# A three-layer kernel on one core: a weight block's conversion moved behind the fourth attention unit, and the second token group's sums ranked later, half of their low parts on VectorE

## The chip, the cores and the metric

The kernel runs on one core of one Trainium2 chip. The metric is the device time of one execution in microseconds (us): the median of three runs.

## What is computed

Attention with a memory term over 2 batches, 8 heads, 576 positions and 64 columns per head, then two feed-forward stages over the 1152 tokens that come out:

```python
scores = scale * np.matmul(q, k.transpose(0, 1, 3, 2))      # causal, softmax -> a
local = np.matmul(a, v)
mem_out = einsum(phi(q), M_prev) / einsum(phi(q), z_prev)
attn = g * mem_out + (1 - g) * local                        # (2, 8, 576, 64)
x = attn.transpose(0, 2, 1, 3).reshape(1152, 512)
h = x @ w_in                                                # 512 -> 2048
x = np.where(h > 0, h, np.exp(np.minimum(h, 0)) - 1) @ w_out
out = 0
for e in range(4):                                          # 512 -> 1024 -> 512 each
    out += p[:, e:e+1] * (np.maximum(x @ w1[e], 0) @ w2[e])
```

## The kernel before

Every float32 product is made of three float32r matmuls (`mm3`, lines 277 to 280): high times high, low times high, high times low. So each operand is split into a high part (a ScalarE copy) and a low part (a subtraction, mostly on GpSimd, which the profile calls POOL).

The tokens are in two groups. Group 0 (384 tokens) comes from four small attention units, `F0` to `F3`, one for each pair of heads. Group 1 (768 tokens) comes from eight larger ones, `R00` to `R13`. `Moe1` and `Moe2` are the two feed-forward stages of group 0. Their matmuls run while the `R` units are still worked out, in gaps of one another. Then `Wide1` and `Wide2` do group 1 with Winograd's scheme of seven products for eight, which needs sums of token quarters (`T1` to `T4`, each in two halves `kk`) and sums of weight quarters (`s32`).

An attention unit makes scores (`sF`, `sR`, banks `s0` and `s1` or `m`), row minima on VectorE (`lowest`, line 1311), exponentials on ScalarE, transposes (`tF`, `tR`), copies of them (`pf`, line 1364 on VectorE), products with the values (`sums`), the scaling of the result (`sum_a`, `sum_i`, `sum_f`: lines 1223, 1438, 1229), the sum with the memory term (`both`, line 1416) and a last transpose (`turn`, tile `xF` or `xR`), which is split into `xh` and `xl`.

A weight block `i` is 128 x 1024. The first sixteen come as 64-bit words, in two halves `w64_i_0` and `w64_i_1`, and are converted: ScalarE `upper` (line 225), VectorE `shift` (231) and `lower` (235), which give the block `wr`. ScalarE then makes its high part `wh` (245), and POOL its low part `wl` (249). The first three blocks are converted in place in `wr`; the others go through the PSUM banks `s0` and `s1` that the scores use too. Those later blocks wait in the plan for `GATE`, one of the scores of `F3` (`score20`). Weight blocks 0 and 1 are for the first upward products (`ua`), 2 and 3 for the first downward ones (`da`).

The order on every engine is set by a planner, `Plan.order`: it plays through the steps with guessed costs, and each time an engine is free takes the step of lowest rank whose inputs and buffers are there. Only the order goes into the program; on the chip each engine runs its queue in that order and waits where it must. Where the planner sees TensorE wait for over 0.3 us in the first 140 us of its own clock, `keep_busy` puts matmuls of zeros (`nothing`, line 304) ahead of the step, into the PSUM tile that the step will write:

```python
waits[0] = min(int(IDLE * wait / 0.22) + 1, IDLE_MAX)
```

The downward results of group 0's first stage share three PSUM banks, tag `m`: of the last part, `da0300`, `da0310` and `da0320` hold all three until VectorE has made their low parts (`yl`, line 457), and `da0330` takes the first that comes free.

Of the kernel before, what the change touches and what calls it, by code (L numbers as in the profile page):

```python
# [54 lines left out]
def f32(ap):  # L55
    return ap.bitcast(F32)
# [3 lines left out]
def tile_kernel(  # L60
# [12 lines left out]
    nc = tc.nc  # L73
# [80 lines left out]
    W_EARLY = 3  # L154
# [14 lines left out]


    FEWEST = {"F": 1, "R": 0}
    GATE = ("F3", "score20")
    UNIT1 = 5.0
    EARLY = 4.0
    START2 = 48.0
    STARTS2 = [0, 35, 70, 95, 110, 125, 140, 155]
# [11 lines left out]
    def plan_weights(plan, i, rank):  # L188

        second, k = divmod(i, NW1 + NW2)  # L190
        t = {}
        last = [None]

        def add(name, engine, cost, fn, takes=(), gives=()):
            plan.add(("w", i, name), engine, cost, rank, fn, [last[0]] if last[0] else (), takes, gives)
            last[0] = ("w", i, name)

        def block():
            t["wr"] = wp.tile([P, 1024], F32, tag="wr", name=f"wr{i}", bufs=SLOTS["wr"])

        def load():
            block()
            if k >= NW1:
                nc.sync.dma_start(out=t["wr"], in_=w32[k - NW1])
            elif second:
                nc.sync.dma_start(out=t["wr"], in_=wscr[k])

        def load64(half):
            cs = slice(512 * half, 512 * half + 512)
            raw = at["sbuf"].tile([P, 512], I64, tag=f"w64_{half}", name=f"w64_{i}_{half}", bufs=SLOTS["w64_0"])  # L210
            nc.sync.dma_start(out=raw, in_=w64[i, :, cs])
            words = raw.bitcast(I32).rearrange("p (n two) -> p n two", two=2)
            t[half] = words[:, :, 0], words[:, :, 1]

        def upper(half):
            if half == 0:
                block()
            _, high = t[half]

            if i < W_EARLY:  # L220
                t["cv", half] = t["wr"][:, 512 * half:512 * half + 512]
            else:
                t["cv", half] = abank(f"s{half}", f"cv{i}_{half}")

            nc.scalar.activation(
                out=t["cv", half], in_=high.bitcast(F32), func=AF.Prelu, scale=2.0 ** -112, alpha=2.0 ** 32
            )

        def shift(half):
            c = t["cv", half].bitcast(I32)  # L230
            nc.vector.tensor_scalar(out=c, in0=c, scalar1=3, scalar2=None, op0=ALU.logical_shift_left)

        def lower(half):
            low, wi = t[half][0], t["wr"][:, 512 * half:512 * half + 512].bitcast(I32)
            nc.vector.scalar_tensor_tensor(
                out=wi, in0=low, scalar=29, in1=t["cv", half].bitcast(I32),
                op0=ALU.logical_shift_right, op1=ALU.bitwise_or,
            )

        def keep():  # L240
            nc.sync.dma_start(out=wscr[i], in_=t["wr"])

        def part_h():
            t["wh"] = wp.tile([P, 1024], F32R, tag="wh", name=f"wh{i}")
            nc.scalar.activation(out=t["wh"], in_=t["wr"], func=AF.Copy)  # L245

        def part_l():
            wl = wp.tile([P, 1024], F32R, tag="wl", name=f"wl{i}")
            nc.gpsimd.tensor_tensor(out=wl, in0=t["wr"], in1=f32(t["wh"]), op=ALU.subtract)  # L249
            wtiles[i] = (t["wh"], wl)  # L250

        if k < NW1 and not second:
            ends = []
            for half in range(2):
                last[0] = None
                add(f"load{half}", "sync", 1.6, lambda half=half: load64(half), [f"w64_{half}"])
                bank = [] if i < W_EARLY else [f"s{half}"]
                plan.add(
                    ("w", i, f"upper{half}"), "act", act_cost(512), rank, lambda half=half: upper(half),
                    [last[0]] + [GATE] * (i >= W_EARLY) + [("w", i, "upper0")] * half, bank + ["wr"] * (half == 0),  # L260
                )
                last[0] = ("w", i, f"upper{half}")
                add(f"shift{half}", "dve", dve_cost(512), lambda half=half: shift(half))
                ends.append(("w", i, f"lower{half}"))
                plan.add(
                    ends[-1], "dve", dve_cost(512), rank, lambda half=half: lower(half), [last[0]], [],
                    [f"w64_{half}", *bank],
                )
            plan.add(("w", i, "keep"), "sync", 1.6, rank + 3.0, keep, [*ends, ("w", i, "part_l")], gives=[("wr", ("w", i, "upper0"))])
            plan.add(("w", i, "part_h"), "act", act_cost(1024), rank, part_h, ends, ["w"])  # L270
            last[0] = ("w", i, "part_h")
        else:
            add("load", "sync", 1.6, load, ["wr"])
            add("part_h", "act", act_cost(1024), part_h, ["w"])
        add("part_l", "pool", pool_cost(1024), part_l, gives=[("wr", ("w", i, "load"))] * (k >= NW1 or second))
# [391 lines left out]
    class Halves:  # L667
# [29 lines left out]
                self.sums[name] = hp[0].tile([P, 2, 384], F32, tag="t32", name=f"{self.what}{name}", bufs=SLOTS["t32"])  # L697
            fn(self.sums[name][:, kk])

        def plan_parts(self, plan, rank, name, kk, gives=()):  # L700
            def high():
                nc.scalar.activation(out=self.tile(name, "h")[:, kk], in_=self.sums[name][:, kk], func=AF.Copy)

            def low():
                nc.gpsimd.tensor_tensor(
                    out=self.tile(name, "l")[:, kk], in0=self.sums[name][:, kk],
                    in1=f32(self.tile(name, "h")[:, kk]), op=ALU.subtract,
                )

            plan.add((self.what, name + "h", kk), "act", act_cost(384), rank, high, [(self.what, name, kk)])  # L710
            plan.add((self.what, name + "l", kk), "pool", pool_cost(384), rank, low, [(self.what, name + "h", kk)], [], gives)

        def plan(self, plan, rank, ready):

            for name, x, y in (("T1", "B12", "B11"), ("T2", "B22", "T1"), ("T3", "B22", "B12"), ("T4", "B21", "T2")):
                for kk in (0, 1):
                    def subtract(out, x=x, y=y, kk=kk):
                        nc.vector.tensor_tensor(
                            out=out, in0=self.quarter(x)[:, kk], in1=self.quarter(y)[:, kk], op=ALU.subtract
                        )  # L720

                    after = [a for n in (x, y) for a in ([(self.what, n, kk)] if n[0] == "T" else ready(n, kk))]
                    plan.add(
                        (self.what, name, kk), "dve", dve_cost(384), rank,
                        lambda name=name, kk=kk, fn=subtract: self.total(name, kk, fn), after, ["t32"] * (kk == 0),
                    )
                    self.plan_parts(plan, rank, name, kk, ["t32"] * kk)

    keep = {}

# [299 lines left out]
    def dve_cost(n):  # L1030
        return 1.042e-3 * n + 0.115

    def pool_cost(n):
        return 2.1e-3 * n + 0.2
# [418 lines left out]
    x1 = Halves("x", lambda: x32)  # L1453
# [12 lines left out]
    with ExitStack() as first, tc.manual_schedule():  # L1466
        attention_pools(attention, first)
        ps_m = first.enter_context(tc.tile_pool(name="ps_m", bufs=SLOTS["m"], space=PSUM, reuse_waits="tile"))

        ps = at["t"].tile([P, 512], F32, tag="t", name="warm")  # L1470
        for i in range(WARM):
            nothing(ps)
        plan, clock = Plan(SLOTS), [START2]
        plan.awake, plan.last = IDLE_END, 0.43 * WARM - 0.5
        plan_small(plan, OFFSET["load"] + 3.0, 1.5)
        for c in range(H // 2):
            plan_unit(plan, "F", None, c, UNIT1 * c, True, {})
        for i in range(W_FIRST):
            plan_weights(plan, i, W_RANKS[i])
        wnext[0] = W_FIRST  # L1480
        units = [(b, c) for c in range(H // 2) for b in (0, 1)]
        for (b, c), start in zip(units, STARTS2):
            plan_unit(plan, "R", b, c, START2 + start, False, {"act": 0.3, "dve": 0.1, "pool": 0.3, "pe": 0.3})
        Moe1(plan, 0, 0, clock).layers()
        Moe2(plan, 0, NW1, clock).layers()
        x1.plan(plan, START2 + STARTS2[-1] + 8.0, lambda name, kk: [(f"R{b}{c}", "join_l") for b, c in units])
        free = plan.order({"pe": 0.43 * WARM - 0.5})
    ps_g = ctx.enter_context(tc.tile_pool(name="ps_g", bufs=8, space=PSUM, reuse_waits="tile"))
    with tc.manual_schedule():
        plan, clock = Plan(SLOTS | {"m": 8, "h": 4}), [free["pe"]]  # L1490
# [91 lines left out]
```

## Time and profile before

| | |
|---|---|
| median of 3 runs | 728.83 us (728.65 to 729.18) |
| the profiled execution | 729.03 us, of which 727.2 us are the span from its first to its last instruction |
| TensorE busy | 717.5 us (99%) |
| VectorE, ScalarE, POOL busy | 396.7, 354.2, 425.7 us |
| mean granted TensorE clock | 0.995 |

Times of rows are microseconds from the span's start. A row of the order of time gives start, duration and, in brackets, the idle time of the engine just before it and who ended it. PE is TensorE, DVE is VectorE, ACT is ScalarE. Tiles stand there without their numbers (`da` for `da0330`, `w` for `w64_2_0`).

### The profile page before, as it was taken

The numbers are of one execution on the slowest core, as the hardware profiler recorded it, in microseconds if no ns is written. First come the engines' busy times: TensorE is split into PE (matmuls) and PEld (weight loads), VectorE is DVE, ScalarE is ACT, GpSimd is POOL, SyncE is SP. The second block draws the span as 40 slices with busy tenths as digits, with TensorE's granted clock in tenths as the row PEclk, the third lists the DMA queues.
The fourth block names the chain that finished last, engine by engine and source line by source line (L and its number), as shares of the span: only waits on it lengthen the run. The fifth ranks groups of instructions, "written<-read, shape, count | busy, mean of one in ns | idle before, by whom it ended". The sixth has DMA issues, their size and how long they took to land.

```text
span 727.2 us, 11034 instructions
## 1 busy us (share of the span) xinstructions
PE 717.5 (99%) x4255; PEld 643.9 (89%) x4255; DVE 396.7 (55%) x846; ACT 354.2 (49%) x610; POOL 425.7 (59%) x256
## 2 busy tenths in 40 slices
PE   9989999999999999998999999999999999999997
PEld 5768998888889888897999999998998989899896
DVE  4887785434353443435537474873635546364562
ACT  7768877454444543444568373753323324243130
POOL 5468688665536442259878763597656456664210
PEclk9999999999999999999999999999999999999999
DMA  7677985434233041221423021112312203021002
GB/s 260 214 267 266 388 294 165 143 106 136 87 108 109 31 138 32 85 91 55 159 88 116 30 87 59 59 33 84 116 40 77 88 29 117 30 88 58 1 1 87
DMA packets 23541, 80.36 MB, mean 110 GB/s; under 512 B 2881, under 2 KB 2881, under 8 KB 23489
## 3 DMA queue, kind: packets, MB, share of 16 engines
q1 hardware_dynamic: 23488, 79.66, 32.6%
q8 instruction: 33, 0.54, 0.3%
q14 instruction: 20, 0.16, 0.1%
HBM read 68.90 MB, written 10.75 MB: 110 GB/s over the span
## 4 chain that ended last, share of the span: by engine, by line
PE 96%; POOL 2%; DVE 1%; issue 0%; ACT 0%
PE db L278 9%; PE db L280 9%; PE db L279 9%; PE sums L1375 5%; PE da L278 5%; PE da L279 5%; PE da L280 5%; PE ub L278 3%; PE sR L1297 3%; PE ub L280 3%; PE ub L279 3%; PE tR L1359 3%; PE sums L1384 2%; PE ua L278 2%; PE ua L280 2%; PE ua L279 2%
## 5 line engine op out<-in xcount | busy, mean ns | idle before, releaser
L249 POOL TENSOR_TENSOR wl<-wr,wh 128x1024 fp32r<-128x1024 f32 x72 | 171.9, 2391 | 178.7 <-ACT wh L245 140.0
L245 ACT ACTIVATE wh<-wr 128x1024 fp32r<-128x1024 f32 x72 | 75.7, 1056 | 96.5 <-PE db L279 55.8
L278 PE MATMUL db<-wh,hb 128*128 128x512 f32 x288 | 115.6, 401 | 0.0
L280 PE MATMUL db<-wl,hb 128*128 128x512 f32 x288 | 113.4, 394 | 2.2 <-POOL wl L249 2.2
L279 PE MATMUL db<-wh,hb 128*128 128x512 f32 x288 | 113.0, 392 | 0.0
L997 DVE SCALAR_TENSOR_TENSOR acc<-db,pr,acc 128x512 f32<-128x512 f32 x42 | 31.5, 751 | 70.0 <-PE db L280 69.2
L280 PEld LDWEIGHTS db<-wl,hb 128*128 128x128 f32 x288 | 54.4, 189 | 14.3 <-POOL wl L249 2.6
L278 PE MATMUL da<-ha,wh 128*128 128x384 f32 x192 | 65.1, 339 | 0.0
L278 PEld LDWEIGHTS db<-wh,hb 128*128 128x128 f32 x288 | 54.5, 189 | 11.9 <-issue 1.4
L280 PE MATMUL da<-ha,wh 128*128 128x384 f32 x192 | 64.2, 334 | 0.0
L279 PE MATMUL da<-ha,wl 128*128 128x384 f32 x192 | 64.2, 334 | 0.0
L279 PEld LDWEIGHTS db<-wh,hb 128*128 128x128 f32 x288 | 54.5, 189 | 10.3
L278 PE MATMUL ub<-yh,wh 128*128 128x384 f32 x128 | 46.3, 362 | 0.0
L280 PE MATMUL ub<-yl,wh 128*128 128x384 f32 x128 | 43.1, 336 | 0.0
L279 PE MATMUL ub<-yh,wl 128*128 128x384 f32 x128 | 43.0, 336 | 0.0
L1375 PE MATMUL sums<-rvR,pfR 128*128 128x65 f32 x288 | 37.4, 271 | 0.0
L278 PEld LDWEIGHTS da<-ha,wh 128*128 128x128 f32 x192 | 36.1, 188 | 0.7 <-issue 0.4
L1375 PEld LDWEIGHTS sums<-rvR,pfR 128*128 128x128 f32 x288 | 35.3, 191 | 1.0
L279 PEld LDWEIGHTS da<-ha,wl 128*128 128x128 f32 x192 | 36.1, 188 | 0.0
L280 PEld LDWEIGHTS da<-ha,wh 128*128 128x128 f32 x192 | 36.0, 188 | 0.0
L537 DVE SCALAR_TENSOR_TENSOR acc<-db,pr,acc 128x512 f32<-128x512 f32 x21 | 15.7, 749 | 36.4 <-PE db L280 36.3
L1320 ACT ACTIVATE ptR<-ptR,nmR 128x576 f32<-128x576 f32 (+2 forms) x48 | 29.9, 659 | 10.2 <-DVE nmR L1311 10.2
(860 smaller groups left out, 1838.1 us busy)
## 6 DMA issues: line engine op xcount, KB each, us to landing
wr<-in_w SPq DMA_DIRECT2D x64, 512.0 KB, 3.5
w<-in_w SPq DMA_DIRECT2D x32, 512.0 KB, 5.8
wscr<-wr SPq DMA_DIRECT2D x16, 512.0 KB, 6.9
wr<-wscr SPq DMA_DIRECT2D x16, 512.0 KB, 3.3
qkR<-in_qk_r SPq DMA_DIRECT2D x8, 480.0 KB, 5.0
rvR<-in_vm_r SPq DMA_DIRECT2D x8, 390.0 KB, 4.0
out<-acc SPq DMA_DIRECT2D x8, 256.0 KB, 2.0
qkF<-in_qk_f SPq DMA_DIRECT2D x4, 416.0 KB, 3.8
```

The source lines that it names most:

```text
L245: nc.scalar.activation(out=t["wh"], in_=t["wr"], func=AF.Copy)
L249: nc.gpsimd.tensor_tensor(out=wl, in0=t["wr"], in1=f32(t["wh"]), op=ALU.subtract)
L278: nc.tensor.matmul(out, ah, bh, start=first, stop=False)
L279: nc.tensor.matmul(out, al, bh, start=False, stop=False)
L280: nc.tensor.matmul(out, ah, bl, start=False, stop=last)
L537: nc.vector.scalar_tensor_tensor(out=acc, in0=t["ps"], scalar=p, in1=acc, op0=ALU.mult, op1=ALU.add)
L997: nc.vector.scalar_tensor_tensor(out=acc, in0=t["ps"], scalar=p, in1=acc, op0=ALU.mult, op1=ALU.add)
L1297: nc.tensor.matmul(unit["s", odd, t, n][:, :w], unit[x][rows, q], unit[y][rows, ks[odd]], start=m == 0 and r0 == 0, stop=m == 2 and final,)
L1320: nc.scalar.activation(out=blk, in_=blk, func=AF.Exp, scale=-1.0, bias=unit["nm"][odd][:, k:k + 1])
L1359: nc.tensor.transpose(pst[:, P * n:P * n + P], src, ident)
L1375: nc.tensor.matmul(unit["ov"][:, odd, t], pf[:, col:col + P], unit["rv"][:, at_], start=j == 0, stop=False)
L1384: nc.tensor.matmul(unit["ov"][r0:r0 + r, o, t], pf[rows, col + r0:col + r0 + r], unit["rv"][rows, at_], start=nb == 0, stop=True,)
```

## The change

Three edits. The third block (`i` is 2, the last that is converted in place) now waits in the plan for `sum_f` of `F3`, where it waited for nothing but its load. The token sums of group 1 get the rank of the end of group 0's layers less 15 (in the planner's clock some 20 us later than before). The low parts of `T1` and `T4` are made on VectorE, and those of `T2` and `T3` stay on POOL. The gates and ranks are only the planner's: no wait is added to the program, but the order of all engines changes from there on, in the first 175 us above all.

```diff
+    GATE_IN_PLACE = ("F3", "sum_f")
...
+                gate = [GATE] if i >= W_EARLY else [GATE_IN_PLACE] if i >= 2 else []
                 plan.add(
                     ("w", i, f"upper{half}"), "act", act_cost(512), rank, lambda half=half: upper(half),
-                    [last[0]] + [GATE] * (i >= W_EARLY) + [("w", i, "upper0")] * half, bank + ["wr"] * (half == 0),
+                    [last[0]] + gate + [("w", i, "upper0")] * half, bank + ["wr"] * (half == 0),
                 )
...
-        def plan_parts(self, plan, rank, name, kk, gives=()):
+        def plan_parts(self, plan, rank, name, kk, gives=(), on_dve=False):
...
+            eng, cost = (nc.vector, ("dve", dve_cost(384))) if on_dve else (nc.gpsimd, ("pool", pool_cost(384)))
...
-                nc.gpsimd.tensor_tensor(
+                eng.tensor_tensor(
                     out=self.tile(name, "l")[:, kk], in0=self.sums[name][:, kk],
...
-                    self.plan_parts(plan, rank, name, kk, ["t32"] * kk)
+                    self.plan_parts(plan, rank, name, kk, ["t32"] * kk, name in ("T1", "T4"))
...
-        x1.plan(plan, START2 + STARTS2[-1] + 8.0, lambda name, kk: [(f"R{b}{c}", "join_l") for b, c in units])
+        x1.plan(plan, clock[0] - 15.0, lambda name, kk: [(f"R{b}{c}", "join_l") for b, c in units])
```

In the listings of the order below, numbers behind the last underscore are the program's buffers, and line numbers after the edit are 1 to 4 higher.

**First place: VectorE at the end of the attention unit `F3`.** Before, a shift of block 2 stands between the scaling of `F3`'s memory term (`nm_F3`) and the copy `pfF31` of its last transposes:

```order
L1229 TENSOR_TENSOR sums_120<-sums_120,nm_F3_633 128x2x3x64
L231 TENSOR_SCALAR wr2_550<-wr2_550 128x512
L1364 COPY pfF31_654<-tF31_644 128x384
L1430 TENSOR_TENSOR xl0_101<-xF2_639,xh0_100 128x384
L235 SCALAR_TENSOR_TENSOR wr2_550<-w64_2_0_371,wr2_550 128x512
L231 TENSOR_SCALAR wr2_550<-wr2_550 128x512
L1223 SCALAR_TENSOR_TENSOR nv_F3_673<-sums_120,wloc_96 128x6
```

After the change:

```order
L1233 TENSOR_TENSOR sums_120<-sums_120,nm_F3_630 128x2x3x64
L1368 COPY pfF31_650<-tF31_640 128x384
L1434 TENSOR_TENSOR xl0_101<-xF2_636,xh0_100 128x384
L1227 SCALAR_TENSOR_TENSOR nv_F3_662<-sums_120,wloc_96 128x6
L1442 RECIPROCAL nv_F3_662<-nv_F3_662 128x6
L1233 TENSOR_TENSOR tvF3_665<-sums_120,nv_F3_662 128x2x3x64
L1420 TENSOR_TENSOR tvF3_665<-tvF3_665,sums_120 128x384
L232 TENSOR_SCALAR wr2_669<-wr2_669 128x512
L236 SCALAR_TENSOR_TENSOR wr2_669<-w64_2_0_371,wr2_669 128x512
```

The copy now follows the scaling at once, and all four instructions of block 2 stand behind `F3`'s `both`.

**Second place: TensorE at the end of group 0's first stage.** Before, `da0330` follows `da0320`, whose last quarter has the inputs `ha033`:

```order
L278 MATMUL da0320_1784<-ha033_1655,wh15_1543 128x384
L279 MATMUL da0320_1784<-ha033_1655,wl15_1547 128x384
L280 MATMUL da0320_1784<-ha033_1655,wh15_1543 128x384
L278 MATMUL da0330_1811<-ha030_1437,wh15_1543 128x384
```

After the change (the pair of zeros is there five times):

```order
L282 MATMUL da0320_1811<-ha033_1719,wh15_1562 128x384
L1301 MATMUL sR01001_1834<-qhR01_1585 128x288
L1301 MATMUL sR01101_1835<-qhR01_1585 128x288
L1301 MATMUL sR01001_1834<-qlR01_1601,qhR01_1585 128x288
L1301 MATMUL sR01101_1835<-qlR01_1601,qhR01_1585 128x288
L1301 MATMUL sR01001_1834<-qhR01_1585,qlR01_1601 128x288
L1301 MATMUL sR01101_1835<-qhR01_1585,qlR01_1601 128x288
L306 LDWEIGHTS zeros_93
L306 MATMUL da0330_1854<-zeros_93 128x384
```

On VectorE the low part of `da0300`, which frees a bank for `da0330`, now stands behind the row minima of those scores:

```order
L448 TENSOR_TENSOR da0300_1777<-da0300_1777,xr0_852 128x384
L448 TENSOR_TENSOR da0310_1798<-da0310_1798,xr0_852 128x384
L448 TENSOR_TENSOR da0320_1811<-da0320_1811,xr0_852 128x384
L1315 ISA ptR01_1745,nmR010_1746<-sR01001_1834,mask_71,nmR010_1746 128x288
L1315 ISA nmR010_1746 128x1
L459 TENSOR_TENSOR yl0_1844<-da0300_1777,yh0_1843 128x384
```

Part of `R01`'s scores moved ahead of `da0330`, and five matmuls of zeros were put there. In all the program has 18 matmuls of zeros behind the first upward product `ua0000` where it had 6: 5 before the scores `sR00001`, 3 before `da0000`, 2 before the scores `sR10000`, 3 before `da0200` and 5 before `da0330`, where it had 4 before `sR00010` and 2 before `ua0100`. The scores' are 512 wide, the others 384.

**Third place: VectorE and POOL at the end of group 0, where the token sums are made.** VectorE before (`acc0` takes group 0's results, `hb071` to `hb073` are the low parts that the last downward products `db070` to `db072` read):

```order
L718 TENSOR_TENSOR xT2_3626<-x32_102,xT1_3609 128x384
L718 TENSOR_TENSOR xT3_3634<-x32_102 128x384 x2
L537 SCALAR_TENSOR_TENSOR acc0_2070<-db061_3616,pr_97,acc0_2070 128x512
L718 TENSOR_TENSOR xT4_3656<-x32_102,xT2_3626 128x384 x2
L537 SCALAR_TENSOR_TENSOR acc0_2070<-db062_3643,pr_97,acc0_2070 128x512
L509 SCALAR_TENSOR_TENSOR hb071_3669<-ub0710_3670,hb071_3669 128x384
```

VectorE after:

```order
L709 TENSOR_TENSOR xT1l_3614<-xT1_3621,xT1h_3613 128x384 x2
L722 TENSOR_TENSOR xT2_3638<-x32_102,xT1_3621 128x384
L539 SCALAR_TENSOR_TENSOR acc0_2087<-db061_3628,pr_97,acc0_2087 128x512
L722 TENSOR_TENSOR xT3_3662<-x32_102 128x384 x2
L722 TENSOR_TENSOR xT4_3667<-x32_102,xT2_3638 128x384 x2
L539 SCALAR_TENSOR_TENSOR acc0_2087<-db062_3650,pr_97,acc0_2087 128x512
L709 TENSOR_TENSOR xT4l_3620<-xT4_3667,xT4h_3619 128x384 x2
L511 SCALAR_TENSOR_TENSOR hb071_3676<-ub0710_3677,hb071_3676 128x384
```

POOL before, up to the low part of the last weight block of group 0, `wl47`:

```order
L705 TENSOR_TENSOR xT1l_3602<-xT1_3609,xT1h_3601 128x384 x2
L705 TENSOR_TENSOR xT2l_3606<-xT2_3626,xT2h_3605 128x384
L601 TENSOR_TENSOR s32_48_0_3787<-wr49_3783 128x512
L705 TENSOR_TENSOR xT2l_3606<-xT2_3626,xT2h_3605 128x384
L705 TENSOR_TENSOR xT3l_3604<-xT3_3634,xT3h_3603 128x384 x2
L601 TENSOR_TENSOR s32_48_0_3787<-s32_48_0_3787,wr48_3781 128x512
L705 TENSOR_TENSOR xT4l_3608<-xT4_3656,xT4h_3607 128x384
L601 TENSOR_TENSOR s32_48_2_3793<-wr48_3781,wr49_3783 128x512
L705 TENSOR_TENSOR xT4l_3608<-xT4_3656,xT4h_3607 128x384
L249 TENSOR_TENSOR wl47_3697<-wr47_3551,wh47_3666 128x1024
```

POOL after:

```order
L709 TENSOR_TENSOR xT2l_3618<-xT2_3638,xT2h_3617 128x384
L603 TENSOR_TENSOR s32_48_0_3799<-wr49_3795 128x512
L709 TENSOR_TENSOR xT2l_3618<-xT2_3638,xT2h_3617 128x384
L603 TENSOR_TENSOR s32_48_0_3799<-s32_48_0_3799,wr48_3793 128x512
L603 TENSOR_TENSOR s32_48_2_3802<-wr48_3793,wr49_3795 128x512
L709 TENSOR_TENSOR xT3l_3616<-xT3_3662,xT3h_3615 128x384 x2
L250 TENSOR_TENSOR wl47_3693<-wr47_3563,wh47_3688 128x1024
```

Four subtractions left POOL ahead of `wl47` and stand on VectorE ahead of `hb071`. On ScalarE the second half of `xT4h` moved behind `wh47` and `wh48A1`, and `hb071`'s high part moved behind `swh48S12`. TensorE's order is the same in both here: `ub0710`, `ub0720`, `ub0730`, then `db070`, which reads `hb070`, `hb071`, `hb072` and `hb073` in turn (three matmuls each), the last two with `wh47` and `wl47`.

## Rows read from the trace of the kernel before

**Rows 1.** All long waits of TensorE: us in total, times, longest.
```profile
PE sums L1375 <- DVE pfF L1364: 2.3, 1, 2.3
PE db L280 <- POOL wl L249: 2.2, 1, 2.2
```
**Rows 2.** Stretches: length, busy us of PE, PEld, DVE, ACT, POOL, then PEclk, DMA, GB/s.
```profile
40.20:43.60 3.40, 3.40 (x19) 1.46 (x18) 3.23 (x8) 0.00 (x0) 0.00 (x0) 0.50 0.47 170
44.00:340.00 296.00, 295.97 (x1904) 261.00 (x1903) 156.05 (x363) 165.37 (x272) 178.57 (x104) 1.00 0.43 144
344.30:347.40 3.10, 3.10 (x9) 2.42 (x8) 0.36 (x1) 1.06 (x1) 3.10 (x3) 0.50 0.54 211
```
**Rows 3.** VectorE in order of time at the end of `F3`.
```profile
37.31 1.74 DVE L231 TENSOR_SCALAR wr<-wr 128x512 int32<-128x512 int32 x1
38.98 0.55 DVE L1364 COPY pfF<-tF 128x384 f32<-128x384 f32 x1
...
40.90 0.16 DVE L1223 SCALAR_TENSOR_TENSOR nv_F<-sums,wloc 128x6 f32<-128x6 f32 x1
...
41.98 0.56 DVE L1416 TENSOR_TENSOR tvF<-tvF,sums 128x384 f32<-128x384 f32 x1
```
**Rows 4.** TensorE in order of time at the same place.
```profile
39.58 0.44 PE L1375 MATMUL sums<-rvF,pfF 128*128 128x65 f32 x2 [2.32 <-DVE pfF L1364]
...
40.76 3.08 PE L304 MATMUL xF<-zeros 128*128 128x512 bf16 x7
43.69 0.49 PE L1422 MATMUL xF<-ident,tvF 128*128 128x128 f32 x3
44.01 0.98 PE L304 MATMUL ua<-zeros 128*128 128x384 bf16 x5
44.69 0.47 PE L278 MATMUL ua<-xh,wh 128*128 128x384 f32 x1
```
**Rows 5.** POOL in order of time: low parts of block 2 and of `R00`'s queries and keys.
```profile
45.73 2.42 POOL L249 TENSOR_TENSOR wl<-wr,wh 128x1024 fp32r<-128x1024 f32 x1 [6.96 <-ACT wh L245]
48.09 2.28 POOL L1179 TENSOR_TENSOR qlR<-qkR,qhR 128x960 fp32r<-128x960 f32 x1
```
**Rows 6.** TensorE: zeros before `sR00010`, and the first downward product `da0000`.
```profile
54.93 1.02 PE L304 MATMUL sR<-zeros 128*128 128x512 bf16 x4
...
59.54 0.35 PE L278 MATMUL da<-ha,wh 128*128 128x384 f32 x1
```
**Rows 7.** VectorE: a low part `yl`, and a row minimum of the scores `sR01001`.
```profile
140.13 0.56 DVE L457 TENSOR_TENSOR yl<-da,yh 128x384 fp32r<-128x384 f32 x1
141.59 0.52 DVE L1311 CUSTOM_DVE_ANT_0 ptR<-sR,mask,nmR 128x288 f32<-128x288 f32 x1 [0.90 <-PE sR L1297]
```
**Rows 8.** TensorE: those scores begin, and what follows them.
```profile
140.88 0.40 PE L1297 MATMUL sR<-qhR 64*128 64x288 f32 x2
...
141.48 0.44 PE L278 MATMUL ub<-yh,wh 128*128 128x384 f32 x1
```
**Rows 9.** POOL where the token sums are made, up to `wl47`.
```profile
329.39 1.33 POOL L705 TENSOR_TENSOR xT2l<-xT,xT2h 128x384 fp32r<-128x384 f32 x1
330.68 1.61 POOL L601 TENSOR_TENSOR s<-wr 128x512 f32<-128x512 f32 x1
...
340.29 2.33 POOL L249 TENSOR_TENSOR wl<-wr,wh 128x1024 fp32r<-128x1024 f32 x1
```
**Rows 10.** VectorE there: token sums alone, and beside POOL.
```profile
326.71 0.55 DVE L718 TENSOR_TENSOR xT<-x,xT 128x384 f32<-128x384 f32 x1
...
328.48 2.65 DVE L718 TENSOR_TENSOR xT<-x 128x384 f32<-128x384 f32 x2
```
**Rows 11.** ScalarE there: the high part `wh47`.
```profile
334.46 1.04 ACT L245 ACTIVATE wh<-wr 128x1024 fp32r<-128x1024 f32 x1
```
**Rows 12.** TensorE: `db070`'s second quarter (with `hb071`) begins, and `db071` begins.
```profile
339.14 0.39 PE L278 MATMUL db<-wh,hb 128*128 128x512 f32 x1
...
343.71 0.39 PE L278 MATMUL db<-wh,hb 128*128 128x512 f32 x1
```

More of the change, by code (lines that the diff above doesn't have):

```diff
@@ L710, in plan_parts @@
             plan.add((self.what, name + "h", kk), "act", act_cost(384), rank, high, [(self.what, name, kk)])
-            plan.add((self.what, name + "l", kk), "pool", pool_cost(384), rank, low, [(self.what, name + "h", kk)], [], gives)
+            plan.add((self.what, name + "l", kk), *cost, rank, low, [(self.what, name + "h", kk)], [], gives)
         def plan(self, plan, rank, ready):
```

## The prediction

> **What bounds the kernel now.** I read the page's busy shares first: TensorE has 717.5 of 727.2 us, so only its idle time and its slow time can be won or lost, and whatever is added to its queue costs its full length. The list of its waits then shows two long ones [rows 1]: 2.3 us at `F3` for VectorE's copy `pfF`, 2.2 us at the end of group 0 for POOL's `wl47`. The windows show that behind each the granted clock was at its lower level: 0.50 for 3.40 and for 3.10 us [rows 2]. Work that takes 3.40 us at 1.2 GHz takes 1.7 at 2.4, so these stretches cost another 1.7 and 1.55 us. Between them TensorE is busy 295.97 of 296.00 us at full clock. So the change can win at most 2.3 + 1.7 + 2.2 + 1.55 = 7.75 us, in two places, and everything that it adds in the 296 us between them is lost. The lists in order of time at these places gave the rest.
>
> My sum is made against the profiled execution, 729.03 us, 0.2 above the median. 0.2% (1.46 us) is about what a measurement can tell from no change.
>
> **Term 1, the third block behind `F3`: -2.9 us.** TensorE stood from 37.26 to 39.58 for `pfF`, whose copy took 0.55 us but sat behind a 1.74 us shift of block 2 [rows 3, 4]. In the new order the copy follows the scaling at once, so it starts where the shift did, 37.31, ends at 37.86, and the sums start 0.05 later as they did before (39.58 after 39.53), at 37.91: 1.67 us earlier. In before the zeros of `xF` began 1.18 us after the sums [rows 4], of which the last 0.56 lay at half clock; at full clock that is 0.9, so they begin at 38.81 and VectorE's chain begins some 0.14 later, near 38.95. This chain (first scaling to the end of `both`) took 40.90 to 42.54, 1.64 us [rows 3], so `both` is ready at 40.6. Before, the transposes `turn` waited not for it but for seven zeros of 3.08 us at half clock, until 43.69 [rows 4]; now the zeros end near 40.1 at full clock and `turn` starts at 40.65, 3.04 earlier. From there to the first upward product were 1.0 us with five zeros; the new order has six, 0.14 more. So it begins at 41.8 instead of 44.69.
>
> This counts on the full clock. Left are idle pieces of about 0.65 (for `pfF`) and 0.5 us (for `both`). Falls are shown behind 2.3 and 2.2 us only [rows 1, 2]; 0.65 is nearer to none than to these, so I take it that the clock stays. The other end is a fall as before, +1.7.
>
> The cover: block 2's conversion is now later, its low part `wl2` stands on POOL behind `R00`'s low part (2.28 us) instead of ahead of it [rows 5], and the first downward product needs it. The two exchange places: `qlR` at 43.65 to 45.9, `wl2` to 48.3. That product ran at 59.54 before [rows 6], here at about 53 as zeros and scores ahead of it move, so 4 us of cover hide the move. Without it each us late would cost one. Block 2's four VectorE instructions now follow `both`, with no stall of TensorE behind them, and SP's loads into its freed 64-bit slots go out about 1 us later, for blocks that are needed over 10 us after they land: nothing.
>
> **Term 2, the new order between 46 and 145 us: +3.2 us.** Zeros are work for TensorE. There are 18 where there were 6. By their rows [rows 4, 6] a 512-wide one takes about 0.25 and a 384-wide one 0.14 where the clock is full (three of the five of 0.98 us lay before the clock rose). New: 7 x 0.25 + 11 x 0.14 = 3.3; old: 4 x 0.25 + 2 x 0.14 = 1.3; so +2.0. It would be nothing where TensorE would have stood in any case; but the 0.03 us of idle in 296 speak against that [rows 2], as the planner put its zeros by guessed waits.
>
> One new wait I expect to be real: before `da0330`. It needs a bank that `yl` of `da0300` frees, and `yl` now stands on VectorE behind the minimum of the scores `sR01001`. In before the scores began at 140.88 and their minimum started 0.71 later, 0.52 long [rows 7, 8]; `yl` takes 0.56. With 0.1 of overlap the bank is free 1.7 us after the scores begin, while TensorE's six score matmuls last 0.6: a wait of 1.1. The five zeros write the same bank, so they stand behind the wait and don't cover it. Another 0.1 is for smaller waits. Who waits behind `da0330` is all of TensorE's queue. Bounds: 0 (zeros all in place of waits and `yl` early) to 4.5.
>
> **Term 3, token sums and lows at the end: -1.0 us.** Before, `wl47` ran on POOL at 340.29 for 2.33 us, to 342.62, and `db071` began at 343.71 [rows 9, 12]. POOL loses four subtractions of 1.33 ahead of it, but they don't come free on VectorE. Token sums took 0.55 alone and 1.33 each beside POOL [rows 10], and the second of that pair ended at 331.13, 0.41 after POOL's instruction ended at 330.72 [rows 9]. So where both engines read two operands from SBUF, they take turns, and a round costs POOL's row, 1.33 for a low part or 1.61 for a weight sum.
>
> Walked through in the new order (an estimate from these rows): VectorE's first `xT1l` starts at 327.8, after the sum that ended at 327.26 and ScalarE's high part (about 0.53, half of the 1.04 for a block twice as wide [rows 11]). The second ends at 329.7, the second half of `xT2` at 331.3, then the four sums `xT3`, `xT4` a round each, at 332.4, 333.8, 335.4 and 336.9, POOL's ends about 1.0 behind each. POOL's `xT3l` is done at 339.1 and `wl47` at 341.7, 0.9 earlier than before. ScalarE makes the second half of `xT4h` behind `wh47` and `wh48A1`, until 338.3, and `swh48S12` and `hb071`'s high part until 339.65. VectorE has `xT4l` done at 338.2 and 339.5, and `hb071` at 340.25. TensorE wants `hb071` at 339.14 [rows 12]. So it waits there 1.15 us, then some 0.25 for `hb072` and 0.1 for `wl47`, 1.5 in all where it was 2.2, and `db071` begins at 342.7 instead of 343.71. The wait goes from POOL's `wl47` to `hb071`. 1.5 is nearer to 2.2 than to none, so the clock falls as before and costs the same.
>
> Behind 350 us TensorE's order is the same; a few exchanges on VectorE and ScalarE I put at nothing, with 0.3 either way, since TensorE's list of waits has no other long row [rows 1].
>
> **Sum.** -2.9 + 3.2 - 1.0 = -0.7: 728.3 from the profiled execution, 728.1 from the median.
>
> **The rivals.**
>
> Faster (B): the clock doesn't fall at 340 us, since the idle time is shorter and split over three places. Then the 1.55 us of slow work go too: 726.6. If some of the new zeros also stand where TensorE would have waited (the lower bound of term 2), 725.4 or less. For it: the wait is shorter than any that a fall followed. Against it: 1.15 us in one piece was not seen without a fall either.
>
> Slower (C): at 331.9 VectorE's first `xT3` and POOL's second `xT2l` come ready 0.06 us apart by my walk. If POOL is first, each of VectorE's sums comes one POOL instruction later, the second half of `xT4h` is ready near 339.5, and `wl47` has begun on POOL at 338.7 and holds VectorE's last `xT4l` for its 2.33 us and the 0.41: to 341.4. Then `hb071`, which stands behind it in VectorE's queue, is ready at 342.25, TensorE stands 3.1 us and `db071` begins at 344.35, 1.65 later than in the forecast: 729.8, and up to 731 with a longer stretch at half clock. It decides from the point where that half of `xT4h` is later than about 339.0. For it speaks a rule, which stands by itself here: the Trainium skill, in "SBUF — State Buffer", section "Who interferes with whom", says that VectorE and GpSimd share a port pair as an exclusive lock, that an instruction of VectorE with two SBUF inputs meets a GpSimd one that reads SBUF, and that whoever issues first keeps it for the whole instruction. By that rule the trace agrees (the 0.41 us after POOL's end), and moving a low part to VectorE leaves the queue for the ports as long as it was: term 3 would then be no gain but for the reordering, and the sum +0.3 instead of -0.7.
>
> No change at the start (D): the half clock comes in spite of the earlier copy, since 1.15 us of idle remain in two pieces. Then term 1 is -1.2: 729.8. Against it: the longer piece is 0.65 us, less than a third of the 2.3.
>
> **How the numbers follow.** Forecast 0.42, B 0.30, C 0.17, D 0.08, others 0.03. The forecast's own range is 727.0 to 729.2, from the bounds of term 2 (it gives +1, or loses 1.3) and the 0.3 of the late part. Taking in most of B and of C gives 725.6 to 730.5. Faster by over 0.2% (below 727.4) is B and a seventh of the forecast: 0.36. Slower (above 730.3) is most of C, half of D where it meets the upper end of term 2, and others: 0.18. The rest, 0.46, is no change that can be measured.
>
> **What would show it.** Term 1: no 1.74 us shift ahead of `pfF`, a wait for it of at most 0.7, the clock at 1.00 from 38 to 44, the first `ua` at about 41.8. A clock of 0.50 there is D. Term 2: 18 zeros behind that at full length, and a wait of about 1.1 at `da0330` for VectorE's `yl`; the whole stretch from the first `ua` to the last `sR` of 46 to 145 us 3.2 longer. If that wait is missing, or the zeros stand where waits were, term 2 is too large. Term 3: waits of TensorE for VectorE's `hb` near 339 instead of for POOL's `wl`; `wl47` done near 341.7; half clock for some 3 us behind it, where full clock is B; VectorE's `xT4l` after 341 is C. Most likely wrong is term 2's wait, which hangs on the moment at which `yl`'s input was ready, and the clock at 340.

## The result, and the profile after

The changed kernel takes 733.76 us (median of four runs, 732.61 to 733.91) against 728.74 for the kernel before in the same session: slower by the ratio 1.0072 (95% interval 1.006 to 1.0084), some 5 us. The forecast was 728.1 and its range ended at 730.5. The profiled execution took 733.79 us, 732.0 of them span, 4.8 more than before.

The list of waits of TensorE in the changed kernel (us in total, times, longest) answers to [rows 1]; it has all rows but those of the first microseconds:

```profile
PE sR L1301 <- DVE wr L236: 1.8, 2, 1.2
PE da L306 <- DVE yl L459: 1.1, 1, 1.1
PE ub L280 <- DVE acc L539: 1.0, 1, 1.0
...
PE sums L1379 <- DVE pfF L1368: 0.7, 1, 0.7
PE xF L1426 <- DVE tvF L1420: 0.4, 1, 0.4
...
PE db L280 <- DVE hb L511: 0.2, 1, 0.2
```

Both long waits are gone. The wait that heads the list now was not forecast: scores `sR` wait for the low halves `wr` of a converted weight block. The windows (length, busy us of PE, PEld, DVE, ACT, POOL, then the granted clock) answer to [rows 2]:

```profile
36.00:41.00 5.00, 3.97 (x32) 2.27 (x30) 3.96 (x10) 2.02 (x5) 1.85 (x1) 1.00 0.72 285
110.20:113.10 2.90, 1.07 (x7) 0.54 (x5) 2.90 (x7) 0.00 (x0) 0.07 (x1) 1.00 0.00 0
114.00:124.00 10.00, 10.00 (x40) 9.45 (x41) 2.45 (x9) 4.53 (x9) 6.70 (x4) 0.50 0.48 154
341.00:349.00 8.00, 6.82 (x36) 5.88 (x35) 7.03 (x8) 5.81 (x10) 8.00 (x6) 1.00 0.01 2
```

The half clock at the start and that at the end have both gone (1.00 in the first and the last row). In their place there are 10 us at 0.50 in the middle, from 114.0 to 124.2, 0.9 us behind the new wait. The page's row of the clock shows the same: one slice of 40 at 7 tenths, the seventh.

Where the 4.8 us come from is read off by first starts of the same tile in both traces:

| stretch | before | after | difference |
|---|---|---|---|
| start to the first scores `sF0000` | 7.26 | 6.61 | -0.65 |
| from there to the first upward product `ua0000` | 37.43 | 34.46 | -2.97 |
| from there to `ub0200` (before at 176.90) | 132.21 | 142.99 | +10.78 |
| from there to `ub0700` | 144.68 | 144.67 | 0.0 |
| from there to `db072` | 26.47 | 24.07 | -2.40 |
| behind it | | | 0.0 |

The first line is not the change's: all the kernels here have the same rows up to there, and their profiles reach the first scores at 6.1 to 7.6 us. Term 1 came as forecast, term 3 better, and the middle cost 10.8 instead of 3.2 us. The rows of the place, TensorE and then VectorE in order of time in the changed kernel:

```profile
110.20 0.60 PE L1363 MATMUL tR<-ident,ptR 128*128 128x128 f32 x4
111.44 0.47 PE L1301 MATMUL sR<-qhR 64*128 64x448 f32 x1 [0.64 <-DVE wr L236]
113.10 0.47 PE L1301 MATMUL sR<-qhR 64*128 64x448 f32 x1 [1.19 <-DVE wr L236]
```
```profile
106.96 0.18 DVE L137 TENSOR_REDUCE prs<-pr 128x9 f32<-128x36 f32 x1
107.17 0.77 DVE L138 TENSOR_SCALAR prs<-prs 128x9 f32<-128x9 f32 x1
107.97 0.22 DVE L139 RECIPROCAL prs<-prs 128x9 f32<-128x9 f32 x1
108.22 2.10 DVE L140 TENSOR_TENSOR pr<-pr,prs 128x36 f32<-128x36 f32 x1
110.25 0.54 DVE L448 TENSOR_TENSOR xr<-da,xr 128x384 f32<-128x384 f32 x1
110.71 0.67 DVE L236 SCALAR_TENSOR_TENSOR wr<-w,cv 128x512 int32<-128x512 int32 x1
111.31 0.68 DVE L232 TENSOR_SCALAR cv<-cv 128x512 int32<-128x512 int32 x1
111.91 0.54 DVE L448 TENSOR_TENSOR xr<-da,xr 128x384 f32<-128x384 f32 x1
112.37 0.67 DVE L236 SCALAR_TENSOR_TENSOR wr<-w,cv 128x512 int32<-128x512 int32 x1
```
POOL at the same time:
```profile
107.87 2.40 POOL L250 TENSOR_TENSOR wl<-wr,wh 128x1024 fp32r<-128x1024 f32 x1
```

The scores are `R10`'s second ones, `sR10010` and `sR10110`, in the banks `s0` and `s1`. Block 15 is being converted in the same two banks, and its second halves on VectorE (`wr`, L236) end at 111.4 and 113.0. They are late because the setting up of the expert probabilities (four small instructions, L137 to L140) stands ahead of them, and of that 2.10 us is one multiply of 36 columns. It ends at 110.32, 0.05 us after POOL's low part of block 14 ended at 110.27. In the kernel before the same multiply took 2.18 us, 0.76 us earlier, and block 15's last half ended at 112.50. But these scores began at 115.45 there, behind more products, and `R10`'s first pair stood behind block 15 (at 112.12 and 112.55), which the new order has at 100.19, ahead of it. Rows of the kernel before, of VectorE and of TensorE:

```profile
107.46 2.18 DVE L140 TENSOR_TENSOR pr<-pr,prs 128x36 f32<-128x36 f32 x1
111.81 0.69 DVE L235 SCALAR_TENSOR_TENSOR wr<-w,cv 128x512 int32<-128x512 int32 x1
```
```profile
115.45 0.47 PE L1297 MATMUL sR<-qhR 64*128 64x448 f32 x2
```

### The profile page after: what moved, and what is told of

The parts are those of the page before. It is cut to its first block, busy times and chain, and to the rows that moved or that the text cites. A ratio compares the mean times of both kernels' runs of the same rounds, so it can differ in the third digit from the quotient of the medians.

```text
span 732.0 us, 11064 instructions
## 1 busy us (share of the span) xinstructions
PE 721.4 (99%) x4267; PEld 648.2 (89%) x4267; DVE 398.6 (54%) x850; ACT 354.4 (48%) x610; POOL 423.5 (58%) x252
## 4 chain that ended last, share of the span: by engine, by line
PE 91%; DVE 4%; ACT 2%; DMA 2%; issue 1%; POOL 0%; SPq 0%; DVEq 0%; ACTq 0%
PE db L280 9%; PE db L282 9%; PE db L281 9%; PE sums L1379 5%; PE da L280 4%; PE da L282 4%; PE da L281 4%; PE ub L280 3%; PE ub L282 3%; PE ub L281 3%; PE sR L1301 3%; PE tR L1363 2%; PE sums L1388 2%; PE sums L1248 1%; DMA wscr<-wr 1%; PE sF L1301 1%
## 5 line engine op out<-in xcount | busy, mean ns | idle before, releaser
L1001 DVE SCALAR_TENSOR_TENSOR acc<-db,pr,acc 128x512 f32<-128x512 f32 x42 | 31.5, 751 | 69.9 <-PE db L282 69.2
L280 PE MATMUL da<-ha,wh 128*128 128x384 f32 x192 | 66.7, 347 | 0.0
L282 PE MATMUL da<-ha,wh 128*128 128x384 f32 x192 | 65.1, 339 | 0.0
L282 PE MATMUL ub<-yl,wh 128*128 128x384 f32 x128 | 43.1, 336 | 0.0
L1379 PE MATMUL sums<-rvR,pfR 128*128 128x65 f32 x288 | 39.3, 279 | 0.2
L1379 PEld LDWEIGHTS sums<-rvR,pfR 128*128 128x128 f32 x288 | 37.0, 199 | 2.2 <-DVE nm_R L1227 0.5
L280 PEld LDWEIGHTS da<-ha,wh 128*128 128x128 f32 x192 | 36.8, 191 | 0.9 <-issue 0.7
L282 PEld LDWEIGHTS da<-ha,wh 128*128 128x128 f32 x192 | 36.8, 191 | 0.0
L1370 ACT ACTIVATE pfR<-tR 128x512 f32<-128x512 f32 x24 | 14.3, 595 | 43.5 <-PE tR L1363 43.5
```

What stands on the lines that cost most here:

```text
L280: nc.tensor.matmul(out, ah, bh, start=first, stop=False)
L282: nc.tensor.matmul(out, ah, bl, start=False, stop=last)
L1001: nc.vector.scalar_tensor_tensor(out=acc, in0=t["ps"], scalar=p, in1=acc, op0=ALU.mult, op1=ALU.add)
L1370: nc.scalar.activation(out=pf[:, :col], in_=unit["t", g][:, :col], func=AF.Copy)
L1379: nc.tensor.matmul(unit["ov"][:, odd, t], pf[:, col:col + P], unit["rv"][:, at_], start=j == 0, stop=False)
```

## The experiments

All ratios are to the kernel before, run in turns on the same chip. Theory A: the loss is this wait and the half clock behind it (1.83 us, and 5.05 for half of the slow stretch's length), with the zeros and the wait at `da0330` besides, and comes from the first edit alone. Theory B: it is spread over the order, or comes from the edits together.

**One edit alone.** With the third edit there, the second moves no row on any engine: a program with the first and third edit has the order of the whole change. Alone it moves one POOL row and one SP row, and it was not run by itself. So the change is the sum of two, and each was run.

The edit of e1_gate_only, against the whole change:

```diff
-        x1.plan(plan, clock[0] - 15.0, ...)
+        x1.plan(plan, START2 + STARTS2[-1] + 8.0, ...)
-                    self.plan_parts(plan, rank, name, kk, ["t32"] * kk, name in ("T1", "T4"))
+                    self.plan_parts(plan, rank, name, kk, ["t32"] * kk)
```


> The third block's gate alone; the token sums' rank and all four low parts stay as before. TensorE's order is that of the whole change up to the end of group 0. Theory A (the loss sits in the middle of the program and comes from this edit alone: a wait of 1.8 us for VectorE at the second scores of R10, some 10 us at half clock behind it, 1.1 us at da0330, 2.0 us of zeros) expects those rows unchanged, the old wait of 2.2 us for wl47 with its half clock at the end, and so the change's time without its gain there: 733.8 + 2.4 = 736.2. Theory B (loss and gain come from the edits together, through when the engines run) expects less than 734.

Measured: 734.19 us, ratio 1.0082 (1.0068 to 1.0096). The same waits stand in the middle (1.9 and 1.1 us) as in the whole change, as theory A has it, and the time is 2.0 us under its 736.2. The old wait for `wl47` is back, but the half clock behind it is not, which is 1.6 us of what is missing:

```profile
349.10 0.50 PE L282 MATMUL db<-wl,hb 128*128 128x512 f32 x1 [2.20 <-POOL wl L250]
```
```profile
349.20:353.00 3.80, 3.80 (x17) 3.13 (x18) 0.75 (x1) 0.81 (x1) 3.80 (x2) 1.00 0.57 207
```

The slow stretch in the middle was shorter too, with a mean clock of 0.57 from 115 to 123 us; from `ua0000` to `ub0200` this run took 141.38 us where the changed kernel took 142.99. The other way go 0.9 us by which its first upward product came later.

The edit of e2_lows_only, against the kernel before:

```diff
+            eng, cost = (nc.vector, ("dve", dve_cost(384))) if on_dve else (nc.gpsimd, ("pool", pool_cost(384)))
...
-                    self.plan_parts(plan, rank, name, kk, ["t32"] * kk)
+                    self.plan_parts(plan, rank, name, kk, ["t32"] * kk, name in ("T1", "T4"))
```


> The low parts of T1 and T4 on VectorE alone; block 2 without its gate, the sums' rank as before (with the low parts moved, the rank makes no difference to the order on any engine). Theory A expects the kernel before up to 330 us, then a short wait for VectorE in place of the 2.2 us for wl47 and full clock behind it: 728.8 - 2.4 = 726.4. Theory B, by which the clock at the end stayed up only because the shifted start let other work fall there: the stretch behind 340 us is again at half clock, 727.8 to 729.

Measured: 726.72 us, ratio 0.9978 (0.9969 to 0.9988): faster by 1.6. TensorE's list of waits shows 2.3 us for `pfF` as before, and at the end 1.0 for `acc` and 0.2 for `hb`; the clock is 1.00 from 43.1 to 720 us. So the third edit is the good one, and the first alone makes the kernel slower.

**The multiply moved to POOL, no order changed.**

The edit of e3_mult_on_pool, against the whole change:

```diff
-        nc.vector.tensor_tensor(out=pr, in0=pr, in1=prs.unsqueeze(2).to_broadcast([P, 9, E]), op=ALU.mult)
+        nc.gpsimd.tensor_tensor(out=pr, in0=pr, in1=prs.unsqueeze(2).to_broadcast([P, 9, E]), op=ALU.mult)
```


> The whole change, every engine's order kept, but the 36-element multiply of the expert probabilities (2.10 us on VectorE, of which most is a stand behind POOL's low part of block 14) is issued to POOL, ahead of that low part. Theory A: VectorE reaches block 15's low parts 2 us earlier, the waits of 0.64 and 1.19 us at R10's second scores shrink to some 0.2 in all, the clock stays at 1.00 from 114 to 124, and the time is 733.8 - 1.6 - 5.05 = 727.1. Theory B (TensorE's clock falls there for another reason, or block 15 is late because of ScalarE or its load): the waits stay over 1 us or the clock falls all the same, 732 or more.

Measured: 727.91 us, ratio 1.0002 (0.999 to 1.0014). Against the changed kernel 5.9 us came back by the medians and 5.1 by the two ratios, with the place of one instruction; in the profiles the stretch from `ua0000` to `ub0200` is 6.5 us shorter (136.49). On POOL it takes 0.25 us, and VectorE's chain no longer stands (this run is some 1.2 us later from its first upward product on):

```profile
109.85 0.25 POOL L140 TENSOR_TENSOR pr<-pr,prs 128x36 f32<-128x36 f32 x1 [0.36 <-PE tR L1363]
```
```profile
109.56 0.21 DVE L139 RECIPROCAL prs<-prs 128x9 f32<-128x9 f32 x1
109.69 0.50 DVE L448 TENSOR_TENSOR xr<-da,xr 128x384 f32<-128x384 f32 x1
110.10 0.68 DVE L236 SCALAR_TENSOR_TENSOR wr<-w,cv 128x512 int32<-128x512 int32 x1
```
```profile
114.00:124.00 10.00, 10.00 (x75) 9.29 (x75) 3.10 (x9) 5.74 (x10) 8.73 (x5) 1.00 0.44 133
```

In the same ten microseconds as above TensorE gets 75 matmuls done where it got 40. The list of waits has none for `wr` any more. Theory A holds here, with 0.8 us less than it asked for. Nine of the eleven executions had a mean granted clock of 1.000; two, of 730.19 and 731.60 us, had 0.995, and where it fell in them is not traced. All four of the changed kernel had 0.992 to 0.994.

**The planner told the cost.** The planner's cost for these four instructions is 1.0; they take 3.3.

The edit of e4_cost_told, against the whole change:

```diff
-        plan.add(("probs",), "dve", 1.0, 30.0, setup_probs, ...)
+        plan.add(("probs",), "dve", 3.3, 30.0, setup_probs, ...)
```


> The whole change, with one number more: the planner is told 3.3 us for setting up the expert probabilities on VectorE where it had 1.0. TensorE's order then differs between 107 and 160 us: R10's second scores stand some 2.6 us later, behind eight more matmuls of da, and the low parts yl stand ahead of the minima of R01's second scores. Theory A: no wait for block 15, none of over 0.3 us at da0330, full clock throughout: 733.8 - 1.8 - 5.05 - 1.1 = 725.9. Theory B: the later scores meet another wait (for the exponentials of R10, or a bank) and the clock falls there: 729 or more.

Measured: 727.63 us, ratio 0.9988 (0.9979 to 0.9997). No wait for `wr`, the clock at 1.00 from 107 to 124. Of the miss against 725.9, 0.9 us is in the middle (135.94 us where 135.0 was asked for): the wait at `da0330`, which I had expected to go since `yl` stands ahead of the minima in this order, stayed at 1.0 us. Another 0.9 stands ahead of the first upward product, where this edit moves nothing. So the minimum alone was not what held `yl`. But VectorE was not free either: another instruction, the scaling `tmR01`, took the minimum's place, and it and the first `yh` of ScalarE both end when `yl` begins (138.14 and 138.08):

```profile
137.59 0.55 DVE L1233 TENSOR_TENSOR tmR<-sums,nm_R 128x384 f32<-128x384 f32 x1
138.11 1.02 DVE L459 TENSOR_TENSOR yl<-da,yh 128x384 fp32r<-128x384 f32 x2
```
```profile
137.61 1.23 ACT L455 ACTIVATE yh<-da 128x384 fp32r<-128x384 f32 x3
```

**The zeros taken out.**

The edit of e5_no_zeros, against e3_mult_on_pool:

```diff
-    IDLE_END = 140.0
+    IDLE_END = 45.0
```


> The kernel with the multiply on POOL, and without the 18 matmuls of zeros behind the first upward product; every engine's order is otherwise the same. Theory A, by which term 2's price for them holds (zeros are plain added work): 727.8 - 3.1 = 724.7. Theory B (they stand where TensorE would have waited anyway): waits of about their length show at the same five places, for the low parts of blocks, for ha or a bank, and the time stays between 727.2 and 728.2. If the clock falls behind such waits, 729 to 731.

Measured: 726.62 us, ratio 0.9972 (0.9962 to 0.9983): 1.3 us less than with the zeros (1.6 in the profiles, from `ua0000` to `ub0200`), between the theories. A wait of their length appears at one of the five places only, the scores `sR00001`, whose 1.18 us of zeros had covered it:

```profile
51.66 0.40 PE L1301 MATMUL sR<-qhR 64*128 64x288 f32 x1
53.04 0.40 PE L1301 MATMUL sR<-qhR 64*128 64x288 f32 x1 [0.98 <-DVE wr L236]
```

Here too scores wait for a block in their bank (block 4). The clock didn't fall behind it.

**ScalarE's order at `da0330`.**

The edit of e6_yh_before_wh19, against e3_mult_on_pool:

```diff
             add("part_h", "act", act_cost(1024), part_h, ["w"])
+            if i == 19:
+                held = list(plan.steps[last[0]])
+                held[4] = [*held[4], ("a0", "d", 3, 2, 0, 2)]
+                plan.steps[last[0]] = tuple(held)
```


> The kernel with the multiply on POOL, and ScalarE's high part of block 19 put behind the three high parts yh of da0300 to da0320, where it stood ahead of them; VectorE's first minimum of R01's second scores moves behind the three yl with it, and two of the five zeros at da0330 go. Theory A (the 1.1 us wait at da0330 is the 1.06 us of wh19 ahead of yh, which yl needs): the wait shrinks to 0.2 or less, 727.8 - 0.9 - 0.3 = 726.6. Theory B, the prediction's (yl waits for the minimum of the scores): the wait shrinks as well, since that minimum has moved too, but then yl would start as soon as the additions on VectorE end, with ScalarE's yh long done. If neither holds, the wait stays near 1.0 and the time at 727.5.

Measured: 726.66 us, ratio 0.9979 (0.997 to 0.9988), 1.25 less than without it, of which 0.3 are the two zeros. The wait shrank from 1.1 to 0.5 us. (The execution that was profiled took 729.95, with a half clock from 17.3 to 24.0 us, ahead of all that this edit moves.) ScalarE's rows, in the changed kernel and in this one:

```profile
143.13 1.06 ACT L246 ACTIVATE wh<-wr 128x1024 fp32r<-128x1024 f32 x1 [4.93 <-issue]
144.10 1.23 ACT L455 ACTIVATE yh<-da 128x384 fp32r<-128x384 f32 x3
```
```profile
140.25 1.53 ACT L459 ACTIVATE yh<-da 128x384 fp32r<-128x384 f32 x3 [4.99 <-DVE da L452]
141.68 1.05 ACT L246 ACTIVATE wh<-wr 128x1024 fp32r<-128x1024 f32 x1
```

VectorE's in the changed kernel:

```profile
144.20 0.52 DVE L1315 CUSTOM_DVE_ANT_0 ptR<-sR,mask,nmR 128x288 f32<-128x288 f32 x1
144.64 0.08 DVE L1315 DVE_READ_ACCUMULATOR2_ANT nmR<- 128x1 f32 x1
144.64 1.48 DVE L459 TENSOR_TENSOR yl<-da,yh 128x384 fp32r<-128x384 f32 x3
```

There `yl` starts at 144.64, when the first `yh` has just ended (144.10 + 0.47, the first of the three) and the minimum too (the next instruction of VectorE starts 0.08 us before its end): both tie. In the run with the planner's cost `tmR01` stood in the minimum's place and the wait stayed; here both queues are clear, since the edit moved the minimum with `wh19`, and the wait halves. What each would have held alone is not shown. What is left is the chain itself: the additions on VectorE (three in a row, 1.61 us) start only when `da0300` is whole, and in this order the last quarters of `da0300`, `da0310` and `da0320` come together.

**A control.**

The edit of e7_before_mult_on_pool, against the kernel before:

```diff
-        nc.vector.tensor_tensor(out=pr, in0=pr, in1=prs.unsqueeze(2).to_broadcast([P, 9, E]), op=ALU.mult)
+        nc.gpsimd.tensor_tensor(out=pr, in0=pr, in1=prs.unsqueeze(2).to_broadcast([P, 9, E]), op=ALU.mult)
```


> The kernel before with nothing changed but the place of the probabilities' multiply, on POOL as in the earlier run. Theory A (the 2.1 us stand of VectorE is there in the kernel before as well, but no score waits behind it, since R10's second scores come 4 us later there): no difference, 728.3 within 0.7. Theory B (the stand costs something wherever it is): about 1 to 2 us faster, 726.5 to 727.3.

Measured: 727.29 us, ratio 0.9984 (0.9973 to 0.9994): a gain of 1.2 us, which is theory B's number, where theory A had none. In the kernel before the first two scores of the pair `sR10001` and `sR10101` start 0.43 us apart (112.12 and 112.55) and here together, and the stretch from `ua0000` to `ub0200` is 0.54 us shorter. A small wait for block 15 was there before as well, too short for a row in the list of waits. The rest looks like the clock's, not the multiply's: five of the 13 executions here had a mean granted clock of 0.998, and four of the 25 beside them of the kernel before. Among these alone the difference is 0.7 us (726.95 against 727.63).

**Mended versions.** Two more, the whole change with the edits of e3, e5 and e6 together, and the third edit with the multiply on POOL without the gate.

> The whole change with the three mends that helped singly: the multiply on POOL, no zeros behind the first upward product, yh ahead of block 19's high part. If the gains add (1.3 and 1.2 from 727.9, less 0.3 that both count): 725.6, with the clock at 1.00 throughout. If a wait grows where the zeros stood (1.0 us at R00's second scores is known) or the clock falls behind one: 726.5 or more.

> The low parts of T1 and T4 on VectorE and the multiply on POOL, without the third block's gate. By the single runs 726.7 - 0.5 to 1.2 = 725.5 to 726.2. Against the run with three mends it tells what the gate is worth once its damage in the middle is mended: 2.9 us won at the start against some 2.7 us that its order still costs in the middle (1.0 at R00's second scores, about 0.5 at da0330, and smaller waits), so within 0.7 of each other.

Measured: 725.87 us, ratio 0.9967 (0.9954 to 0.9979), and 726.15 us, ratio 0.9973 (0.9963 to 0.9984), both within 0.3 us of what was expected if the gains add. Both are faster than the kernel before and than the changed one, and their intervals overlap, so with its damage mended the gate of the third block is worth nothing that these runs can tell.

## Why the prediction was wrong

**Right: term 1, by its own steps.** No shift stands ahead of `pfF`, TensorE waits 0.66 us for it (0.65 forecast) and 0.36 for `both` (0.5), the clock stays at 1.00, and from the first scores to the first upward product it is 2.97 us shorter (2.9). The rows that answer to [rows 4]:

```profile
37.00 0.44 PE L1379 MATMUL sums<-rvF,pfF 128*128 128x65 f32 x2 [0.66 <-DVE pfF L1368]
...
38.01 1.47 PE L306 MATMUL xF<-zeros 128*128 128x512 bf16 x6
39.84 0.55 PE L1426 MATMUL xF<-ident,tvF 128*128 128x128 f32 x3 [0.36 <-DVE tvF L1420]
```

**Wrong: term 2, at the step "One new wait I expect to be real: before `da0330` ... Another 0.1 is for smaller waits".** There was a second one, at `R10`'s second scores, of 1.83 us, with 10 us of half clock behind it that cost some 5.05 more. Together 6.9 of the 7.6 us by which the middle was mis-sized; with the multiply on POOL the middle is 6.5 us shorter and costs 4.3 where 3.2 was forecast. The step failed in method: I looked at what the tiles that TensorE needs are made of, and at the banks `m`, but not at who else holds `s0` and `s1` at the moment to which the scores had moved. In the traces these scores begin 4.0 us earlier (115.45, then 111.44), while block 15's halves end 0.5 to 0.7 us later (110.70 and 112.50, then 111.38 and 113.04). The order had the scores moved, and the profile before already showed the 2.18 us multiply on VectorE ahead of those halves.

The two terms that I did price came out at their size: the zeros of the middle took 3.12 us against 1.15 before (+1.97, forecast +2.0), and the wait at `da0330` 1.09 (forecast 1.1). But the zeros were not all additional, since without them 1.0 us of wait came back in one place and 1.3 us was gained. And the wait's cause was put in one queue only: the prediction had the minimum of `sR01001` on VectorE, and ScalarE's `wh19` ahead of `yh` held it as long. That the size came out all the same is luck in part.

**Term 3: right place, too small.** It gave -2.4 for -1.0. The wait fell to 1.2 us, as 0.98 for VectorE's `acc` and 0.2 for `hb071`, and the clock didn't fall; a lasting clock is the condition of rival B, which said -2.55 in all. The walk had `hb071` as the late one. It was `acc0` of `db062`, which stood behind 3.2 us of token sums and frees the bank that `ub0730` needs:

```profile
340.74 3.21 DVE L722 TENSOR_TENSOR xT<-x,xT 128x384 f32<-128x384 f32 x2
343.87 0.74 DVE L539 SCALAR_TENSOR_TENSOR acc<-db,pr,acc 128x512 f32<-128x512 f32 x1
...
346.61 0.56 DVE L511 SCALAR_TENSOR_TENSOR hb<-ub,hb 128x384 fp32r<-128x384 f32 x1
```

The two sums take 1.6 us each beside POOL's weight sum of 1.60 (0.54 alone), as [rows 9, 10] had it.

**The rivals.** B's condition held, and its gain was real (the third edit alone made the kernel 1.6 us faster), but it was hidden by a loss elsewhere. C didn't occur: `xT4l` ended at 346.5, with `wl47` begun at 346.06, and POOL's `wl47` was not waited for. D didn't occur (the clock at 1.00 from 36 to 41). None of them was at the place of the loss, and the chance of 0.18 for slower was for the wrong reason.

## What to carry to other kernels

A reordering of TensorE has to be checked against every holder of the PSUM banks that a moved matmul writes, at its new moment: list what else is in that bank, and follow the release back through its engine's queue to something that is late. An instruction of 36 columns can be the late one: here it took 2.10 us on VectorE beside a long one of POOL, and 0.25 us on POOL itself. Moving it there brought back 5 to 6 us and left the scores where they were. And where one missed wait of under 2 us was followed by 10 us of half clock, the range should carry that price, some 5 us.

## What the runs showed of the hardware

**A small instruction on VectorE stood until a long one of POOL had ended.** The multiply of 36 columns, with both inputs in SBUF, took 2.10 us on VectorE beside `wl14` and ended 0.05 us after it, and 0.25 us on POOL. In the five profiles that have it on VectorE it took 2.09 to 2.18 us. The Trainium skill says in "SBUF — State Buffer", section "Who interferes with whom", that a VectorE instruction with two inputs in SBUF and a GpSimd instruction that reads SBUF contend for an exclusive lock, held for the whole instruction. By that rule the trace agrees, with the 0.05 us. The prediction had weighed it at the end of group 0 only. Less expected is the addition of a constant to nine columns (L138) just ahead of it, which reads one operand and took 0.77 us in the changed kernel. It ended at 107.94, 0.03 us after POOL's `ha` of 106.89, and took 0.17 us in the kernel before, where POOL stood idle at that moment.

**The same wait doesn't always bring the half clock.** The wait of 2.2 us for `wl47` was followed by 3.1 us at 0.50 in the kernel before [rows 2], and by a full clock in the runs e1 and e7. The stretch is not of one length either. Behind the 2.3 us for `pfF` it was 3.40 us in the kernel before and 6.7 in the run e7, and behind 1.83 us it was 10 us in the changed kernel and 6.6 in e1. The rows are e7's, behind `pfF` and behind `wl47`:

```profile
41.30:48.00 6.70, 5.94 (x27) 3.33 (x28) 4.79 (x11) 0.42 (x2) 0.00 (x0) 0.50 0.54 187
345.80:350.00 4.20, 4.20 (x18) 3.49 (x19) 0.99 (x2) 1.06 (x1) 4.20 (x2) 1.00 0.52 187
```

The 1.83 us were two waits, of 0.64 and 1.19 us with one matmul between them; right behind a single wait of 0.65 to 1.1 us no profile here has a fall. But two falls stand behind no long wait at all: in e6 from 17.3 to 24.0 us, and in e7 from 24.2 to 30.8, where the longest wait of TensorE since 8 us was one of 0.52 us, 3 and 11 us earlier (e6's row):

```profile
17.30:24.00 6.70, 6.70 (x40) 4.71 (x39) 3.91 (x13) 4.29 (x9) 3.33 (x3) 0.50 0.67 214
```

What decides between these is open, and so a change of 2 or 3 us in a single execution of this kernel can be the clock's alone.
